# Linear attention and a tanh-shrink MLP on one core: batch 1 inside layer 2 of chunk 0 regrouped, kv on packed v, its last tokens in chunk 1

## The chip, the cores and the metric

The kernel runs on one core of one Trainium2 chip. The core has engines that run side by side, each with its own in-order queue: PE (matmuls; PEld is its weight load), DVE (vector), ACT (scalar and activation), POOL (GpSimd) and SP (which here only issues DMAs). POOL issues DMAs too. The metric is the device time of one execution in microseconds. The kernel before takes 285.66 us, the median of three runs (285.46 to 286.16).

## The reference

Inputs q, k and v have the shape (8 batches, 8 heads, 576 tokens, 64). Linear attention with phi(x) = elu(x) + 1 is followed by a two-layer MLP with g = h - tanh(h):

```python
q_p, k_p = (phi(q), phi(k))
kv  = einsum('bhsd,bhse->bhde', k_p, v)          # 64 x 64 for each head
z   = sum(k_p, axis=2)                           # 64 for each head
num = einsum('bhsd,bhde->bhse', q_p, kv)
den = einsum('bhsd,bhd->bhs', q_p, z)[..., None] + 1e-06
x   = (num / den) as (4608 tokens, 512)
h   = x @ w_in                                   # 512 x 2048
out = (h - tanh(h)) @ w_out                      # 2048 x 512
```

## The kernel before, in words

**Tiles.** The 4608 tokens are worked through in nine chunks `c` of 512. A chunk has layer 1 (16 tiles `fi` of 128 hidden features, four matmuls of 128x512 each, L425) and layer 2 (four blocks of 128 tokens, sixteen matmuls each, L446). After a pair of layer-1 tiles ACT takes the tanh (L431) and DVE subtracts (L432, into `gT`); in chunk 0 this is done for single tiles (L436, L437). ACT copies a finished layer-2 block out of PSUM (`evac`, L455) and SP stores it (L466). A batch has 576 tokens, so chunks and batches don't line up: chunk 1 holds tokens 512 to 1023, which are the last 64 tokens of batch 0 and the first 448 of batch 1; chunk 2 begins with the last 128 of batch 1.

**Attention.** For a batch, phi of q and k is an exponential on ACT (L131), a `max, add` on DVE (L132) and a minimum on DVE (L133), twice for each tensor (i = 0, 1, pairs of heads). q is then transposed, by PE through `ident` for batches 0 and 1 (L161, copied out by ACT L165 and DVE L167), by a DMA on SP for the later ones (L150). kv is 72 matmuls in 64x64 tiles (`kv_mm`, L179). z comes with it as further columns: for batch 1 (`a_kv`, L182) the moving operand is a 64-column piece of v and a 64-column piece of ones, which lie in a third slot of `v_b[1]` (128 columns, written by the POOL memset L484); for the batches from 2 on (`kv_cols_mm`, L194) it is a packed copy `vp` of v, 64 columns of v and two of ones (66 columns), made by DVE (`a_vp`, L192). `kz_copy` (or the end of `a_kv`) takes kv and the masked z to SBUF on DVE. `a_den` makes the denominators (16 matmuls L330, an add L335 and a reciprocal L339 on DVE). `num_mm` (L267) makes the numerators of the first 512 tokens of a batch, in 64x512, and `rest_mm` (L275) those of the last 64, in 64x64.

**Scaling by 1/den.** The reciprocals are spread over the partitions. Batch 0 does this with fp32 selection matmuls (L294) for the first 512 tokens and with a round trip through DRAM for its last 64 (`b0_rest`: four stores and two broadcast loads on SP, L307 and L310; `scale_rest`, L317). Batch 1 splits the reciprocals into bf16 parts on DVE (`a_split`, L349 to L352), spreads all 576 by bf16 selection matmuls (`a_spread_pe`, L413) in two halves, and multiplies (`a_scale`, L418) with the numerators, which ACT has copied to `ns` (L584 for the last 64 tokens, L588). Batch 2 goes through DRAM (`a_spread`, L359, L362), the later batches scale q itself.

**What sets the order.** The order of each engine's work is the order of the calls, written out by hand. `s1[fi]` and `s2[s]` are lists of things to do after layer-1 tile `fi` and after layer-2 step `s` of a chunk. In layer 2 of chunk 0 a step `s` is `(g, i) = divmod(s, 4)`: group g of four features, step i; a step has four matmuls. The loads of q, k and v are issued on POOL (L91), and since `kraw` and `qraw` have one buffer, the next batch's load waits until phi of the present one has read it. All eight PSUM banks are one tile, `ps_all`; layer 2 of chunk 0 accumulates in banks 0 to 3, so that batch 1 has banks 4 to 7; layer 1 of chunk 1 takes banks `fi % 6`. The steps that matter here, in chunk 0:

```python
s2[4]  a_qphi(1, 1), load_q(2), load_k(2), load_v(2)
s2[7]  a_qT_pe(1, 0, banks 4, 5), a_kv(1, 6), a_qT_pe(1, 1, banks 4, 5)
s2[8]  scale_rest(0, 6, ..), a_den(1, 4), num1(), a_split(1)
s2[10] spread1(0)
s2[11] exp2(q of batch 2, half 0)
s2[12] spread1(1), exp2(q, half 1), rest2(q, half 0)
s2[13] exp2(k, half 0), rest2(q, half 1), a_qT_dma(2)
s2[14] rest2(k, half 0)
```

`exp2` is the exponential on ACT and `rest2` the two DVE steps. After steps 12 to 15 comes the `evac` of a finished block, ahead of the things in the list. In layer 1 of chunk 1: `s1[0]` a gate on POOL (L442) that waits for the transposed q of batch 2, and the loads of batch 3; `s1[1]` phi of the second half of k; `s1[3]` `a_vp(2, ..)`; `s1[8]` `kv_cols_mm(2, 6, 0)` and `kz_copy(2, 6, 0)` (L202, L207); `s1[10]` `a_den(2, 6)` and `a_spread(2)`.

Of the kernel before, what the change touches and what calls it, by code (L numbers as in the profile page):

```python
# [12 lines left out]
BF16 = mybir.dt.bfloat16  # L13
# [5 lines left out]
def kernel(  # L19
# [9 lines left out]
    nc = tc.nc  # L29
    B, H, S, D = q.shape  # L30
# [43 lines left out]
    w_out_sb = const.tile([128, NF, DM], BF16, name="w_out_sb")  # L74
    kz_c = [const.tile([128, 2, 2, 96], BF16, name=f"kz{i}") for i in range(2)]

    v_b = [const.tile([128, 3, 2, J, D], BF16, name=f"v{i}") for i in range(2)]
    vp = const.tile([128, 2, J, 2, 66], BF16, name="vp")


# [2 lines left out]
    def load(b, t, src, halves):  # L83

        x = src[b].rearrange("h (p j) d -> (h p) (j d)", j=J)
        if halves:
            for i in range(2):
                nc.gpsimd.dma_start(out=t[:, :, i].rearrange("q h j d -> q h (j d)"),  # L88
                                    in_=x.rearrange("(h i q) x -> i q h x", h=2, i=2)[i])
        else:  # L90
            nc.gpsimd.dma_start(out=t.rearrange("q h i j d -> q (h i) (j d)"),  # L91
                                in_=x.rearrange("(n q) x -> q n x", n=4))
# [5 lines left out]
    def load_q(b):  # L98
        q_t[b] = kpool.tile([128, 2, 2, J, D], BF16, name="qraw")
        load(b, q_t[b], q, b == 0)  # L100

    def load_v(b):
        load(b, v_b[b % 2][:, 0:2], v, b == 0)

    def load_wi(f0, n):

# [35 lines left out]
    def a_qphi(b, i):  # L142
        phi(b, q_t, qp_t, "qp", i)
# [29 lines left out]
    def kv_mm(b, v_of, ps_of):  # L173

        kp = kp_t[b]
        for i in range(2):
            for j in range(J):
                for rs, cs, hg, h in quads():
                    nc.tensor.matmul(ps_of(cs, hg, i), kp[rs, i, j, h, :], v_of(rs, h, i, j),  # L179
                                     start=(j == 0), stop=(j == J - 1))  # L180

    def a_kv(b, b0):  # L182

        kz_t[b], vt = kz_c[b % 2], v_b[b % 2]
        kv_mm(b, lambda rs, h, i, j: vt[rs, h:3:2 - h, i, j, :],
              lambda cs, hg, i: ps_all[cs, b0 + hg, 128 * i:128 * i + 128].rearrange("p (a e) -> p a e", a=2))
        ps = ps_all[:, b0:b0 + 2, 0:256].rearrange("p g (i e) -> p g i e", i=2)
        nc.vector.tensor_mul(kz_t[b][:, :, :, 64:96], ps[:, :, :, 64:96], mask)
        nc.vector.tensor_copy(kz_t[b][:, :, :, 0:64], ps[:, :, :, 0:64])

    def a_vp(b, i):
        nc.vector.tensor_copy(vp[:, i, :, :, 0:64].rearrange("p j h d -> p h j d"), v_b[b % 2][:, 0:2, i])  # L192

    def kv_cols_mm(b, b0, o):  # L194
        kz_t[b] = kz_c[b % 2]
# [104 lines left out]
            ns[:, p, j0:j1].rearrange("p j (t c) -> p t j c", t=4),  # L300
            ps_all[:, 4:8, 128 * n + 16 * j0:128 * n + 16 * j1].rearrange("p t (j c) -> p t j c", c=16))

    def b0_rest():

        ds = dram.tile([H, 4, 16], F32, name="ds0")
        for t in range(4):
            nc.sync.dma_start(out=ds[:, t, :], in_=rden_t[0][32 * t:32 * t + H, 128:144])  # L307
        rdb = rpool.tile([128, NP, 4, 16], F32, name="rdb0")
        for hh in range(2):
            nc.sync.dma_start(  # L310
                out=rdb[64 * hh:64 * hh + 64].rearrange("p a t c -> p (a t c)"),
                in_=ds[4 * hh:4 * hh + 4].rearrange("h t c -> (h t c)").partition_broadcast(64))
        rdb_t[0] = rdb

    def scale_rest(b, b0, rdb):
        for h, ps in enumerate(rest_mm(b, b0, 0)):
            nc.vector.tensor_mul(  # L317
                xT[:, 2 * h:2 * h + 2, S * b + 512:S * b + 576].rearrange("p a (t c) -> p a t c", t=4),
                ps.rearrange("p a (t c) -> p a t c", t=4), rdb[:, 2 * h:2 * h + 2])
# [84 lines left out]

        return rpool.tile([128, NP, J, 64], F32, name="ns", tag="rdb")

    def a_spread_pe(b, bank0, pairs):

        bp = ps_all[:, bank0:bank0 + 4, :]
        for n, p in enumerate(pairs):  # L410
            for t in range(4):
                r = slice(32 * t, 32 * t + 32)
                nc.tensor.matmul(bp[:, t, 144 * n:144 * n + 144], sel3[r, p].rearrange("p h e -> p (h e)"),  # L413
                                 rden_t[b][r], start=True, stop=True)
        return bp

    def a_scale(b, p, ns, bp, o):
        nc.vector.tensor_mul(  # L418
            xT[:, p, S * b:S * b + S].rearrange("p (j t c) -> p t j c", j=J, t=4),
            ns[:, p].rearrange("p j (t c) -> p t j c", t=4),  # L420
            bp[:, :, o:o + 144].rearrange("p t (j c) -> p t j c", c=16))


    def l1mm(c, fi, h, p, n):
# [24 lines left out]
    def evac(c, i, o, f0=0, f1=None):  # L449
        f1 = DM if f1 is None else f1  # L450
        osb = opool.tile([128, DM], F32, name="osb")
        if f0:
            nc.vector.tensor_copy(osb[:, f0:f1], o[:, f0:f1])  # L453
        else:
            nc.scalar.copy(osb[:, f0:f1], o[:, f0:f1])  # L455

        if c == NC - 1 and i == 3:
            nc.sync.dma_start(
                out=out[(B - 1) * S:, f0:f1].rearrange("(p j) m -> p j m", j=J)[:, J - 2:J],
                in_=osb[:, f0:f1])  # L460
            return
        for half in range(2):
            b, j = divmod(2 * (4 * c + i) + half, J)
            cuts = [f0, 256, f1] if c == 3 and i < 3 else [f0, f1]
            for a0, a1 in zip(cuts, cuts[1:]):
                nc.sync.dma_start(  # L466
                    out=out[b * S:(b + 1) * S, a0:a1].rearrange("(p j) m -> p j m", j=J)[:, j, :],
                    in_=osb[64 * half:64 * half + 64, a0:a1])
# [12 lines left out]
    load_wo(0)  # L481
    load_wo(1)
    load_q(1)
    nc.gpsimd.memset(v_b[1][:, 2], 1.0)  # L484
    nc.gpsimd.memset(vp[:, :, :, :, 64:66], 1.0)
    load_v(1)
    for n in range(2):
# [51 lines left out]
    b0_kz(0)  # L539
    a_den(0, 4)  # L540
    ns0 = new_ns(0)
    b0_rest()
    b0_num(0)
    b0_kv(1)
    b0_kz(1)
# [22 lines left out]
    for c in range(NC):  # L568
# [4 lines left out]
        if c == 0:  # L573
            sub = {}

            def spread1(h):
                sub["bp"] = a_spread_pe(1, 4, (2 * h, 2 * h + 1))
                for p in (2 * h, 2 * h + 1):
                    a_scale(1, p, sub["ns"], sub["bp"], 144 * (p % 2))

            def num1():
                ns = sub["ns"] = new_ns(1)
                for h, ps in enumerate(rest_mm(1, 6, 128)):
                    nc.scalar.copy(ns[:, 2 * h:2 * h + 2, 8, :], ps)  # L584
                for i in range(2):
                    b0 = 4 + 2 * i
                    num_mm(1, i, lambda h: b0 + h)
                    nc.scalar.copy(ns[:, i::2, 0:8, :].rearrange("p a j t -> p a (j t)"), ps_all[:, b0:b0 + 2, :])  # L588

            s1[11].append(lambda: a_kphi(1, 0))  # L590
            s1[13].append(lambda: a_kphi(1, 1))
            s2[3].append(lambda: a_qphi(1, 0))
            s2[4].append(lambda: (a_qphi(1, 1), load_q(2), load_k(2), load_v(2)))
            s2[0].append(prepare)
            s2[7].append(lambda: (a_qT_pe(1, 0, Banks([4, 5])), a_kv(1, 6), a_qT_pe(1, 1, Banks([4, 5]))))
            s2[8].append(lambda: (scale_rest(0, 6, rdb_t[0]), a_den(1, 4), num1(), a_split(1)))
            s2[10].append(lambda: spread1(0))

            qs, ks = [], []

            def exp2(pieces, src, store, name, i):
                pieces.append(phi_pieces(2, src, store, name, i))
                pieces[i][0]()

            def rest2(f):
                f[1]()
                f[2]()

            s2[11].append(lambda: exp2(qs, q_t, qp_t, "qp", 0))
            s2[12].append(lambda: (spread1(1), exp2(qs, q_t, qp_t, "qp", 1), rest2(qs[0])))  # L610
            s2[13].append(lambda: (exp2(ks, k_t, kp_t, "kp", 0), rest2(qs[1]), a_qT_dma(2)))
            s2[14].append(lambda: rest2(ks[0]))
        elif n1 < B:
            if c == 1:
                s1[8].append(lambda: (kv_cols_mm(2, 6, 0), kz_copy(2, 6, 0)))
            if n1 < QS:
                s1[10].append(lambda: (a_den(n1, 6), a_spread(n1)))
            else:
                if c == 2:
                    s1[2].append(lambda: (q_den(n1, 0, 0), q_den(n1, 0, 1)))  # L620
                e = 2 * (c == 2)
                s1[3 + e].append(lambda: q_den(n1, 1, 0))
                s1[5 + e].append(lambda: q_den(n1, 1, 1))
                s1[7 + e].append(lambda: q_scale(n1))
            m = 12 if c == 1 else 9
            s2[m].append(lambda: a_num(n1, n2 if n2 < B else 0))
            if n2 < B:
                s2[m + 2].append(lambda: (q_zb(n2, 4 if c == 1 else 7), q_prod(n2)))
                if c > 1:
                    s2[15].append(lambda: (q_den(n2, 0, 0), q_den(n2, 0, 1)))  # L630
# [100 lines left out]
```

## Time and profile before

| what | value |
|---|---|
| median of three runs | 285.66 us |
| profiled execution, its own time | 285.88 us |
| span in its profile | 284.1 us |
| PE busy | 277.1 us, 98% |
| DVE busy | 175.8 us, 62% |
| ACT busy | 146.6 us, 52% |
| POOL busy | 74.1 us, 26% |
| granted PE clock | full speed in every slice |
| L446 and L425, layers 2 and 1 | 560 matmuls each, 124.6 and 122.7 us busy |
| L179, kv of batch 1 (128 columns) / of a later batch (66) | 72 matmuls: 1.13 us / 0.71 us in the chain |
| L484, memset of the ones beside v | 1.08 us on POOL |

The span is the profiled execution from its first to its last instruction; what lies around it, 1.8 us here, is the difference to its own time. A "busy" share is an average over the whole span. A chain of work that ended last is followed back from the end, so a stretch of it that names one engine without gaps says that this engine set the pace there. Lines such as `L446` are lines of the kernel before; in the tables of groups, the number behind "x" counts instructions.

### The profile page before, as it was taken

Reading aid. Unit: us, or ns where it says so; the run is one execution under the profiler, and the core shown is the slowest. Engines: PE = TensorE matmul, PEld = TensorE weight load, DVE = VectorE, ACT = ScalarE, POOL = GpSimd, SP = SyncE. Lnnn points to the kernel's source line nnn. Section 1 sums busy time; section 2 is a strip of 40 time slices with the busy share of each in tenths; the row PEclk is TensorE's granted clock in tenths of the full one; section 3 lists DMA queues with packets and bytes.
Section 4 is the critical chain, followed back from the end, with each engine's and each line's share of the span. In section 5 each row is a group of like instructions: output and inputs, shape, how many; then the busy total and the mean of one; then the engine's idle time right before and its main releaser. Section 6 shows DMA issues by size and latency. Waiting matters only on the chain.

```text
span 284.1 us, 5104 instructions
## 1 busy us (share of the span) xinstructions
PE 277.1 (98%) x2099; PEld 131.8 (46%) x2099; DVE 175.8 (62%) x279; ACT 146.6 (52%) x179; POOL 74.1 (26%) x66
## 2 busy tenths in 40 slices
PE   8879999999999999999999999999999999999995
PEld 3564464444444454445444444444444444444443
DVE  5748977997479773976397648764770267006600
ACT  3738658847445663667355736663551355126411
POOL 8652030020360536143605360505050000000000
PEclk9999999999999999999999999999999999999999
DMA  6999999997992299037913693141105210230032
GB/s 99 192 206 213 207 207 207 245 171 141 228 234 69 52 203 221 9 85 131 235 34 70 109 223 85 40 111 45 37 16 119 61 37 2 52 79 18 2 74 74
DMA packets 38343, 32.99 MB, mean 116 GB/s; under 512 B 16016, under 2 KB 34096, under 8 KB 38192
## 3 DMA queue, kind: packets, MB, share of 16 engines
q0 software_dynamic: 17488, 18.35, 39.9%
q1 hardware_dynamic: 20832, 14.31, 20.0%
q8 instruction: 16, 0.26, 0.4%
q14 instruction: 7, 0.06, 0.1%
HBM read 38.01 MB, written 9.46 MB: 167 GB/s over the span
## 4 chain that ended last, share of the span: by engine, by line
PE 90%; DMA 5%; POOL 1%; DVE 1%; ACT 1%; issue 1%; SPq 0%; DVEq 0%; POOLq 0%
PE ps_all L425 43%; PE ps_all L446 40%; DMA v<-in_v_dram 3%; DMA out_dram<-osb 2%; PE ps_all L179 2%; PE ps_all L267 2%; PE ps_all L653 1%; DVE xT L298 1%; ACT osb L455 1%; SPq L466 0%; POOL kraw L88 0%; POOL qraw L88 0%; PE ps_all L330 0%; PE ps_all L294 0%; PE ps_all L161 0%
## 5 line engine op out<-in xcount | busy, mean ns | idle before, releaser
L446 PE MATMUL ps_all<-w_out_sb,gT 128*128 128x512 bf16 x560 | 124.6, 379 | 0.0
L425 PE MATMUL ps_all<-xT,w_in_sb 128*128 128x512 bf16 x560 | 122.7, 379 | 0.0
L432 DVE TENSOR_TENSOR gT<-ps_all,th 128x1024 bf16<-128x1024 f32 x64 | 77.7, 1217 | 46.7 <-ACT th L431 46.7
L431 ACT ACTIVATE th<-ps_all 128x1024 f32<-128x1024 f32 x64 | 65.6, 1024 | 48.2 <-PE ps_all L425 47.5
L425 PEld LDWEIGHTS <-w_in_sb 128*128 128x128 bf16 x560 | 54.6, 98 | 65.6
L446 PEld LDWEIGHTS <-gT 128*128 128x128 bf16 x560 | 53.8, 98 | 63.3 <-issue 0.2
L455 ACT COPY osb<-ps_all 128x512 f32<-128x512 f32 (+1 forms) x36 | 20.9, 583 | 56.4 <-PE ps_all L446 42.2
L238 POOL TENSOR_TENSOR qp<-qp,rd 128x1152 bf16<-128x1152 bf16 x10 | 21.0, 2117 | 39.1 <-issue 23.7
L224 POOL TENSOR_TENSOR pr<-qp,zb 128x1152 f32<-128x1152 bf16 x10 | 23.4, 2359 | 23.9 <-ACT zb L217 23.9
L131 ACT ACTIVATE e<-qraw 128x1152 bf16<-128x1152 bf16 x16 | 18.5, 1160 | 7.0 <-DMA qraw<-in_q_dram 7.0
L229 DVE TENSOR_REDUCE dn<-pr 128x9 f32<-128x576 f32 x20 | 14.5, 745 | 12.2 <-POOL pr L224 12.2
L131 ACT ACTIVATE e<-kraw 128x1152 bf16<-128x1152 bf16 x15 | 17.4, 1162 | 0.4 <-DMA kraw<-in_k_dram 0.4
L133 DVE TENSOR_TENSOR qp<-e,r 128x1152 bf16<-128x1152 bf16 x16 | 12.1, 758 | 4.9 <-ACT e L131 4.1
L133 DVE TENSOR_TENSOR kp<-e,r 128x1152 bf16<-128x1152 bf16 x15 | 11.4, 758 | 6.1 <-ACT e L131 5.1
L91 POOL DMA_DIRECT2D kraw<-in_k_dram x7 | 5.4, 770 | 28.9 <-ACT e L131 26.2
L437 DVE TENSOR_TENSOR gT<-ps_all,th 128x512 bf16<-128x512 f32 x16 | 10.3, 685 | 3.1 <-ACT th L436 2.5
L436 ACT ACTIVATE th<-ps_all 128x512 f32<-128x512 f32 x16 | 9.2, 598 | 5.7 <-PE ps_all L653 4.5
L91 POOL DMA_DIRECT2D qraw<-in_q_dram x7 | 5.4, 768 | 23.8 <-DVE r L132 13.3
L517 PE MATMUL ps_all<-zero 128*128 128x512 bf16 x29 | 8.9, 466 | 1.2 <-DVE zero L471 1.2
L132 DVE TENSOR_SCALAR r<-qraw 128x1152 bf16<-128x1152 bf16 x16 | 7.4, 461 | 0.5 <-DMA qraw<-in_q_dram 0.5
L453 DVE COPY osb<-ps_all 128x128 f32<-128x128 f32 x1 | 0.3, 291 | 11.6 <-DMA out_dram<-osb 11.6
L132 DVE TENSOR_SCALAR r<-kraw 128x1152 bf16<-128x1152 bf16 x15 | 6.8, 451 | 0.0
(103 smaller groups left out, 137.7 us busy)
## 6 DMA issues: line engine op xcount, KB each, us to landing
out_dram<-osb SPq DMA_DIRECT2D x64, 128.0 KB, 2.4
kraw<-in_k_dram POOLq DMA_DIRECT2D x7, 576.0 KB, 6.5
qraw<-in_q_dram POOLq DMA_DIRECT2D x7, 576.0 KB, 8.4
v<-in_v_dram POOLq DMA_DIRECT2D x7, 576.0 KB, 11.3
w_in_sb<-in_moe_w_in_dram POOLq DMA_DIRECT2D x3, 512.0 KB, 13.7
w_out_sb<-in_moe_w_out_dram POOLq DMA_DIRECT2D x3, 512.0 KB, 18.7
rdb<-ds SPq DMA_DIRECT2D x2, 576.0 KB, 7.8
out_dram<-osb SPq DMA_DIRECT2D x13, 64.0 KB, 4.4
```

What stands on the lines that cost most here:

```text
L91: nc.gpsimd.dma_start(out=t.rearrange("q h i j d -> q (h i) (j d)"), in_=x.rearrange("(n q) x -> q n x", n=4))
L131: return (lambda: nc.scalar.activation(e, x, AF.Exp), lambda: nc.vector.tensor_scalar(r, x, 0.0, 1.0, ALU.max, ALU.add), lambda: nc.vector ...
L132: lambda: nc.vector.tensor_scalar(r, x, 0.0, 1.0, ALU.max, ALU.add),
L133: lambda: nc.vector.tensor_tensor(y, e, r, ALU.min))
L224: nc.gpsimd.tensor_mul(pr_t[b][:, i].rearrange("p j h d -> p j (h d)"), qp_t[b][:, i].rearrange("p j h d -> p j (h d)"), zb_t[b][:, i].uns ...
L229: nc.vector.tensor_reduce(dn_t[b][:, i, :, h], pr_t[b][:, i, :, h, :], mybir.AxisListType.X, ALU.add)
L238: nc.gpsimd.tensor_mul(x, x, rd[:, i].unsqueeze(2).to_broadcast([128, J * 2, D]))
L425: nc.tensor.matmul(h, w_in_sb[:, p, fi * 128:(fi + 1) * 128], xT[:, p, c * 512:(c + 1) * 512], start=(n == 0), stop=(n == NP - 1))
L431: nc.scalar.activation(th, h, AF.Tanh)
L432: nc.vector.tensor_sub(gT[:, fi:fi + 2, :], h, th)
L446: nc.tensor.matmul(o, gT[:, fi, i * 128:(i + 1) * 128], w_out_sb[:, fi, :], start=(fi == 0), stop=(fi == NF - 1))
L455: nc.scalar.copy(osb[:, f0:f1], o[:, f0:f1])
```

## The change

Batch 1's work inside layer 2 of chunk 0 is regrouped. Both halves of q are transposed in one go (into banks 4, 5 and 6, 7). kv then runs on packed v (`vp`, 66 columns) in banks 4 and 5, as it does for the later batches; the packing is done by two copies on POOL, in the step that holds the loads of batch 2 and ahead of them in POOL's queue. The third slot of `v_b` and its memset go. Batch 0's last 64 tokens are multiplied right behind this kv, in other columns of the same banks. den and num of batch 1 stand together in step 8, num with its second half first. Batch 1's last 64 tokens are no longer computed here: their reciprocals go through DRAM (`spread_rest(1)`, six DMAs on SP, as for batch 0), and their matmuls and scaling stand beside kv of batch 2 in chunk 1. The spread is one block of 16 matmuls of 128 columns after step 11, where there were two of 8 with 144 columns after steps 10 and 12. In chunk 3 the store of the last block is cut in two column halves as those of the other blocks are.

```diff
-    v_b = [const.tile([128, 3, 2, J, D], BF16, name=f"v{i}") for i in range(2)]
+    v_b = [const.tile([128, 2, 2, J, D], BF16, name=f"v{i}") for i in range(2)]
...
-    def a_kv(b, b0):
...
-    def a_vp(b, i):
-        nc.vector.tensor_copy(vp[:, i, :, :, 0:64].rearrange("p j h d -> p h j d"), v_b[b % 2][:, 0:2, i])
+    def a_vp(b, i, eng=nc.vector):
+        eng.tensor_copy(vp[:, i, :, :, 0:64].rearrange("p j h d -> p h j d"), v_b[b % 2][:, :, i])
...
-    def b0_rest():
+    def spread_rest(b):
...
-            nc.sync.dma_start(out=ds[:, t, :], in_=rden_t[0][32 * t:32 * t + H, 128:144])
+            nc.sync.dma_start(out=ds[:, t, :], in_=rden_t[b][32 * t:32 * t + H, 128:144])
...
-    def scale_rest(b, b0, rdb):
-        for h, ps in enumerate(rest_mm(b, b0, 0)):
+    def scale_rest(b, pss):
+        rdb = rdb_t[b]
+        for h, ps in enumerate(pss):
...
-    def a_spread_pe(b, bank0, pairs):
+    def a_spread_pe(b, pairs):
...
-                nc.tensor.matmul(bp[:, t, 144 * n:144 * n + 144], sel3[r, p].rearrange("p h e -> p (h e)"),
-                                 rden_t[b][r], start=True, stop=True)
+                nc.tensor.matmul(ps_all[:, 4 + t, 128 * n:128 * n + 128], sel3[r, p].rearrange("p h e -> p (h e)"),
+                                 rden_t[b][r, 0:128], start=True, stop=True)
...
-            cuts = [f0, 256, f1] if c == 3 and i < 3 else [f0, f1]
+            cuts = [f0, 256, f1] if c == 3 else [f0, f1]
...
-    nc.gpsimd.memset(v_b[1][:, 2], 1.0)
...
-            def spread1(h):
-                sub["bp"] = a_spread_pe(1, 4, (2 * h, 2 * h + 1))
-                for p in (2 * h, 2 * h + 1):
-                    a_scale(1, p, sub["ns"], sub["bp"], 144 * (p % 2))
+            def spread1():
+                a_spread_pe(1, range(NP))
+                for p in range(NP):
+                    a_scale(1, p, sub["ns"], p)
+
+            def kv1():
+                kv_cols_mm(1, 4, 0)
+                pss = rest_mm(0, 4, 256)
+                kz_copy(1, 4, 0)
+                scale_rest(0, pss)
...
-                for h, ps in enumerate(rest_mm(1, 6, 128)):
-                    nc.scalar.copy(ns[:, 2 * h:2 * h + 2, 8, :], ps)
-                for i in range(2):
+                for i in (1, 0):
...
-            s2[4].append(lambda: (a_qphi(1, 1), load_q(2), load_k(2), load_v(2)))
+            s2[4].append(lambda: (a_qphi(1, 1), a_vp(1, 0, nc.gpsimd), a_vp(1, 1, nc.gpsimd), load_q(2), load_k(2), load_v(2)))
...
-            s2[7].append(lambda: (a_qT_pe(1, 0, Banks([4, 5])), a_kv(1, 6), a_qT_pe(1, 1, Banks([4, 5]))))
-            s2[8].append(lambda: (scale_rest(0, 6, rdb_t[0]), a_den(1, 4), num1(), a_split(1)))
-            s2[10].append(lambda: spread1(0))
+            s2[7].append(lambda: (a_qT_pe(1, 0, Banks([4, 5])), a_qT_pe(1, 1, Banks([6, 7])), kv1()))
+            s2[8].append(lambda: (a_den(1, 4), num1(), spread_rest(1), a_split(1)))
+            s2[11].append(spread1)
...
-            s2[12].append(lambda: (spread1(1), exp2(qs, q_t, qp_t, "qp", 1), rest2(qs[0])))
+            s2[12].append(lambda: (exp2(qs, q_t, qp_t, "qp", 1), rest2(qs[0])))
...
-                s1[8].append(lambda: (kv_cols_mm(2, 6, 0), kz_copy(2, 6, 0)))
+                def kv2():
+                    kv_cols_mm(2, 6, 0)
+                    pss = rest_mm(1, 6, 256)
+                    kz_copy(2, 6, 0)
+                    scale_rest(1, pss)
+
+                s1[8].append(kv2)
```

More of the change, by code (lines that the diff above doesn't have):

```diff
@@ L102, in load_v @@
     def load_v(b):
-        load(b, v_b[b % 2][:, 0:2], v, b == 0)
+        load(b, v_b[b % 2], v, b == 0)
     def load_wi(f0, n):
@@ L180, in kv_mm @@
                                      start=(j == 0), stop=(j == J - 1))
-    def a_kv(b, b0):
[L184 to L189, printed above, removed]
-    def a_vp(b, i):
-        nc.vector.tensor_copy(vp[:, i, :, :, 0:64].rearrange("p j h d -> p h j d"), v_b[b % 2][:, 0:2, i])
+    def a_vp(b, i, eng=nc.vector):
+        eng.tensor_copy(vp[:, i, :, :, 0:64].rearrange("p j h d -> p h j d"), v_b[b % 2][:, :, i])
     def kv_cols_mm(b, b0, o):
@@ L312, in b0_rest @@
                 in_=ds[4 * hh:4 * hh + 4].rearrange("h t c -> (h t c)").partition_broadcast(64))
-        rdb_t[0] = rdb
-    def scale_rest(b, b0, rdb):
-        for h, ps in enumerate(rest_mm(b, b0, 0)):
+        rdb_t[b] = rdb
+    def scale_rest(b, pss):
+        rdb = rdb_t[b]
+        for h, ps in enumerate(pss):
             nc.vector.tensor_mul(
@@ L405, in new_ns @@
         return rpool.tile([128, NP, J, 64], F32, name="ns", tag="rdb")
-    def a_spread_pe(b, bank0, pairs):
-        bp = ps_all[:, bank0:bank0 + 4, :]
+    def a_spread_pe(b, pairs):
         for n, p in enumerate(pairs):
@@ L412, in a_spread_pe, with a_scale @@
                 r = slice(32 * t, 32 * t + 32)
-                nc.tensor.matmul(bp[:, t, 144 * n:144 * n + 144], sel3[r, p].rearrange("p h e -> p (h e)"),
-                                 rden_t[b][r], start=True, stop=True)
-        return bp
-    def a_scale(b, p, ns, bp, o):
+                nc.tensor.matmul(ps_all[:, 4 + t, 128 * n:128 * n + 128], sel3[r, p].rearrange("p h e -> p (h e)"),
+                                 rden_t[b][r, 0:128], start=True, stop=True)
+    def a_scale(b, p, ns, n):
         nc.vector.tensor_mul(
-            xT[:, p, S * b:S * b + S].rearrange("p (j t c) -> p t j c", j=J, t=4),
-            ns[:, p].rearrange("p j (t c) -> p t j c", t=4),
-            bp[:, :, o:o + 144].rearrange("p t (j c) -> p t j c", c=16))
+            xT[:, p, S * b:S * b + 512].rearrange("p (j t c) -> p t j c", j=8, t=4),
+            ns[:, p, 0:8].rearrange("p j (t c) -> p t j c", t=4),
+            ps_all[:, 4:8, 128 * n:128 * n + 128].rearrange("p t (j c) -> p t j c", c=16))
     def l1mm(c, fi, h, p, n):
@@ L541 @@
     ns0 = new_ns(0)
-    b0_rest()
+    spread_rest(0)
     b0_num(0)
```

## The prediction, made before the change was run

> **What bounds the kernel now.** I read the page's busy rows first, then the chain of work that ended last, in order of time, around the edited blocks, then the timeline of all engines there, and last the DMA issues with their landings.
>
> ```profile
> PE   8879999999999999999999999999999999999995
> ...
> PE 90%; DMA 5%; POOL 1%; DVE 1%; ACT 1%; issue 1%; SPq 0%; DVEq 0%; POOLq 0%
> ```
>
> PE is busy in every slice but the first few, and the chain is PE for 90% of the span: from 21 us on, PE work taken away shortens the kernel, unless a wait takes its place. The chain through the edited stretch (start, length, what):
>
> ```profile
> 38.55 0.50 PE ps_all L161 x9
> 39.05 1.13 PE ps_all L179 x72
> 40.18 0.61 PE ps_all L161 x9
> 40.79 0.86 PE ps_all L446 x4
> 41.66 0.19 PE ps_all L275 x8
> 41.84 0.36 PE ps_all L330 x16
> ...
> 42.43 0.25 PE ps_all L275 x7
> 42.69 0.92 PE ps_all L267 x8
> 43.61 1.83 PE ps_all L446 x8
> 45.44 0.24 PE ps_all L413 x8
> 45.67 1.83 PE ps_all L446 x8
> 47.51 0.24 PE ps_all L413 x8
> 47.74 2.70 PE ps_all L446 x12
> ```
>
> The reader is to see the seven interruptions of L446 (layer 2) and what each costs. But PE is not alone here. In the timeline (start, length, engine, and in brackets the idle time before and its releaser) the other engines stand close behind:
>
> ```profile
> 38.64 0.74 POOL L91 DMA_DIRECT2D qraw<-in_q_dram  x1 [13.29 <-DVE r L132]
> 46.34 1.16 ACT L131 ACTIVATE e<-qraw 128x1152 bf16<-128x1152 bf16 x1 [1.27 <-DMA qraw<-in_q_dram]
> 50.62 1.07 ACT L455 COPY osb<-ps_all 128x512 f32<-128x512 f32 x2
> 52.20 1.02 ACT L431 ACTIVATE th<-ps_all 128x1024 f32<-128x1024 f32 x1 [0.51 <-PE ps_all L425]
> 53.26 1.22 DVE L432 TENSOR_TENSOR gT<-ps_all,th 128x1024 bf16<-128x1024 f32 x1 [0.35 <-ACT th L431]
> 60.14 0.41 DVE L207 CAST kz<-ps_all 128x256 bf16<-128x256 f32 x1
> 60.68 0.43 PE L330 MATMUL ps_all<-qT,kz 128*32 128x144 bf16 x16
> ```
>
> ACT waits for q of batch 2, issued at 38.64 and landing at 46.24 (7.6 us). From 46.34 it works without a gap to 51.69 (5.35 us: three exponentials, four evacuations), then idles only 0.51 us before chunk 1's first tanh. That releases DVE at 53.26, which has no gap until kz of batch 2 is done at 60.55; PE's den of batch 2 starts 0.13 us later. So this second chain has 0.51 us of room at the tanh, and about 0.1 us at den.
>
> **PE's work.** A layer-2 matmul takes 6.91/32 = 0.216 us. From 38.55 to 50.44 stand 32 of them, 6.91 of 11.89 us; the blocks cost 4.98. After the change: 18 transposes in one run, 2 x 0.50 = 1.00 (the 0.61 held a switch); kv on packed v, 72 of 66 columns, 0.71 (the L179 block at 58.21 in chunk 1); eight rest matmuls beside it, 0.06 (between 77.15 and 77.21); den 0.36; num 0.56 (the eight at 76.76; here they now take 0.92, with waits); one spread. Eight of 144 columns take 0.24, of which 2 groups x 144 x 0.00042 = 0.12 is columns (0.216/512 each), so sixteen of 128 take 0.12 + 4 x 0.054 = 0.34. Three returns to layer 2 cost 1.83 - 8 x 0.216 = 0.10 each. Sum 1.00 + 0.77 + 0.92 + 0.34 + 0.30 = 3.33, a saving of 1.65; batch 1's rest in chunk 1 gives back 0.06. PE alone: **-1.59 us**.
>
> **What the packed v adds.** Two copies of 128x1152 on POOL now stand between v's landing and kv, and ahead of the issue of q, k and v of batch 2 in POOL's queue. v of batch 1, issued at 17.05, lands 21.2 us later, at 38.25. Dropping the memset (1.08 us at 15.96) moves its issue up by a microsecond but not its landing: transfers on this queue land in order, 576 KB every 2.84 us (q 35.43, v 38.25), at 207 GB/s in every slice here. So POOL cannot start before 38.3, and PE, which began kv at 39.05, is to read the copies.
>
> No POOL copy of this size is in the trace. Below stands the memset of the same size, 1.08 us, which writes and reads nothing; above the POOL product of the same size (L238), 2.12, which reads two inputs. I take 1.1, nearer the memset because a copy reads one stream, and keep both ends. The start: DVE's minimum (L133) runs 38.22 to 38.98 with both inputs in SBUF. The nearest row on sharing is DVE's copy of v (L192): median 0.454, but 0.58 at 71.38 and 0.65 at 100.47, each beside a POOL DMA issue. I take 0.2 us of delay (bounds 0 and 0.7): start 38.45, copies done 39.55 and 40.65.
>
> The Trainium skill (SBUF — State Buffer, "Who interferes with whom") says that a VectorE instruction with two SBUF inputs and a GpSimd one that reads SBUF exclude each other for the whole instruction; by it the copies would start at 38.98 and the end be 286.5. The Trainium skill (GPSIMD Engine Reference, 3.1) gives 1.8 cycles an element at 1.2 GHz for a tight loop, an estimate of 1.73 us a copy, and the end 287.2; its 4.1 calls one-input work roughly line-rate, as the memset row has it. No run here shows either yet.
>
> PE: transposes end at 39.55; first half of kv to 40.0; the second half waits for 40.7. That stall of 0.7 us, and 0.1 before num's last half (bank 4 is read by den's add, behind two scalings on DVE), leave 0.8 of the 1.59.
>
> **What follows from POOL.** q's issue starts at 40.65 plus 0.34, the gap after a POOL copy (55.87 + 0.18 to 56.39): 41.0, not 38.64. Behind it in the queue are k and v of batch 2. An issue that finds the queue empty lands 6.2 us later (k of batch 3, 56.39); q of batch 0 in halves, 4.6 + 1.4 for the second half's bytes, gives 6.0. With 6.1, q lands at 47.1; the queue's order would have allowed 46.24 (weights until 43.4, plus 2.84). So the delay is 0.9 us. ACT's 5.35 us then run 47.2 to 52.55, the tanh starts at 52.6 (0.4 late), DVE's chain ends 0.4 late, and den of batch 2, with its 0.1 of room, starts **0.3 us later** than now, whatever PE saved ahead of it. Nothing gives this back: after den PE runs without idle time to the end.
>
> With d for one copy, the end moves by 2d - 1.9 us, and by no less than -0.6: q cannot land before 46.24, which leaves 0.5 at the tanh and 0.1 at den.
>
> **The rest.** The two scalings moved to chunk 1 (2 x 0.285 on DVE, behind kz) meet 0.43 us of idle time before the next subtraction, so 0.14 us is late, and later idle times of 0.32 and 0.50 take it; without that cover 0.57. The six small DMAs of the rest go to SP near 43.8. Its pair of batch 0 waited 3.5 us between stores and loads, and took 6.4 in all, so SP is free at 50.2 rather than 48.2. Behind it queue four output stores and the transpose of q (51.76), perhaps 1 us late. That holds the gate on POOL (55.87) and the loads of batch 3; q transposed is read at 60.68 and would land at 56.7; v of batch 3 (68.84, read at 69.00) would hold DVE 0.9 us where it later idles 0.89. Nothing for PE. ACT's two small copies of rest (0.43) go from a stretch in which it then waits 1.27. Two more stores in chunk 3 meet an SP that mostly waits. The scaling, 4 x 0.68 after a spread at 45.8, ends by 48.8, before chunk 1's layer 1.
>
> **Sum.** The profiled execution took 285.88 us (span 284.1). Plus 0.3 is 286.18; it stands 0.22 above the median of 285.66, so the forecast is **286.0**. A measurement can tell about 0.3% (0.86 us) from no change.
>
> **Rivals.** (A) The forecast: PE's saving is eaten by the later q, through ACT and DVE. With d 1.1, its ends come from start 38.3 to 38.98, gap 0 to 0.34, landing 5.7 to 6.2: from the floor of -0.6 (285.1) to +0.9 (286.5). Chance 0.55, within. (B) Slower: POOL's copies are slow, like its products. It decides from d = 1.4, where 2d - 1.9 passes 0.86; at 1.7 it is +1.5 (287.2), at 2.12 +2.3 (288.0); 287.6 in the middle. For it: every POOL arithmetic row is near 2 us; against: the memset. Chance 0.33, slower. (C) Faster: DVE and ACT run ahead and PE's saving comes through, 285.66 - 1.59 = 284.1. It needs q no later than now and 1 us that DVE's gapless stretch doesn't show. Chance 0.08. (D) The copies' reads hold DVE's minimum and the work behind it for a whole copy, 1.1 us on the path to transposes and so to kv, and the scalings in chunk 1 lose their cover, 0.14: 286.9. Chance 0.04, slower.
>
> The range leaves out C and the upper edge of B, and takes in the floor of A: 285.0 to 287.9. A alone: 285.1 to 286.5. Faster 0.08, same 0.55, slower 0.37.
>
> **What will show it.** In the changed profile: two POOL copies near 38.4, with their length; kv's second half held by them; the issue of q near 41.0 and its landing near 47.1; no idle time of ACT before the first tanh, at 52.6; den of batch 2 held by DVE's kz. Layer 2 of chunk 0 is to end near 49.7, 0.8 sooner than now, and this gain is to be gone at den. Wrong would be copies of another length, a q that lands as before, or PE keeping its gain past 61 us.

## The result and the profile after

The changed kernel takes **287.1 us** (median of 22 runs, 285.5 to 288.6), the kernel before, run beside it, 285.81 (22 runs). The ratio is 1.0044, with a 95% interval of 1.0033 to 1.0056: 1.3 us slower. The profiled execution has a span of 285.4 us, 284.1 before. The measured time lies in the stated range of 285.0 to 287.9, but above the 286.5 at which the forecast's own rival (A) ended, and it is slower by more than 0.3%, where "within 0.3%" was held likeliest.

Line numbers of the kernel after differ: layer 1 is L415 (before L425), layer 2 L436 (L446), the evacuation L445 (L455), the tanh L421 (L431), the subtraction L422 (L432), the copy of v L183 (L192), kz L193 and L198 (L202, L207), the scaling of a batch's last 64 tokens L309 (L317), den L322 (L330), num L258 (L267), the spread L404 (L413).

The page of the changed kernel, first PE's busy tenths in 40 slices, then the chain that ended last:

```profile
PE   8879989899999999999999999999999999999995
...
PE 77%; DMA 10%; issue 6%; POOL 3%; ACT 2%; SPq 0%; DVE 0%; POOLq 0%; ACTq 0%
```

A digit is PE's busy share of one slice in tenths. Two slices (36 to 43 us and 50 to 57 us) fell from 9 to 8, and the chain has gone over to DMA and POOL for part of the way. The chain between 38 and 62 us says where (start, length, what):

```profile
38.39 0.08 POOL vp L183
...
39.96 1.09 POOL vp L183
41.05 7.26 DMA qraw<-in_q_dram
...
48.40 1.16 ACT e L131
49.56 0.47 ACT osb L445
50.03 1.06 ACT e L131
...
51.46 1.17 ACT e L131
52.64 0.48 ACT osb L445
...
53.16 6.20 PE ps_all L415 x28
```

It is to be read from the top: copies of v on POOL, the load of q issued behind them, ACT's exponentials and evacuations, and only then layer 1 on PE. The same stretch in the timeline (in brackets the idle time before, and its releaser):

```profile
38.39 2.71 POOL L183 COPY vp<-v 128x1152 bf16<-128x1152 bf16 x2 [12.93 <-DMA v<-in_v_dram]
41.05 0.74 POOL L91 DMA_DIRECT2D qraw<-in_q_dram  x1
48.40 1.16 ACT L131 ACTIVATE e<-qraw 128x1152 bf16<-128x1152 bf16 x1 [2.94 <-DMA qraw<-in_q_dram]
53.47 1.05 ACT L421 ACTIVATE th<-ps_all 128x1024 f32<-128x1024 f32 x1
40.07 0.48 PE L179 MATMUL ps_all<-vp,kp 64*64 64x66 bf16 x36 [0.32 <-POOL vp L183]
41.16 0.48 PE L179 MATMUL ps_all<-vp,kp 64*64 64x66 bf16 x36 [0.61 <-POOL vp L183]
50.38 1.03 PE L415 MATMUL ps_all<-xT,w_in_sb 128*128 128x512 bf16 x4
51.62 1.02 PE L415 MATMUL ps_all<-xT,w_in_sb 128*128 128x512 bf16 x4 [0.22 <-ACT osb L445]
53.16 6.20 PE L415 MATMUL ps_all<-xT,w_in_sb 128*128 128x512 bf16 x28 [0.52 <-ACT osb L445]
61.26 0.41 DVE L198 CAST kz<-ps_all 128x256 bf16<-128x256 f32 x1
61.59 0.48 DVE L309 TENSOR_TENSOR xT<-ps_all,rdb 128x128 bf16<-128x128 f32 x2
61.93 0.43 PE L322 MATMUL ps_all<-qT,kz 128*32 128x144 bf16 x16
```

q was issued at 41.05 (38.64 before) and landed at 48.31 (46.24). ACT's first tanh of chunk 1 starts at 53.47 (52.20), without idle time ahead of it. On PE the account is short. Transposes start at 38.41 (38.39 before), layer 1 at 50.38 (50.28): up to here the regrouping has won nothing. From layer 1 to den of batch 2 it is 11.55 us against 10.40. The eight matmuls from 50.38 to 53.16 take 2.78 us where 8 x 0.216 = 1.73 is their work, so **1.05 us** is waiting for ACT to empty banks 1 and 2; the rest of batch 1 is some 0.06. Together with the later start of layer 1 (0.10) that is 1.2; den is 1.25 us late, the span 1.3. From den to the end the two kernels take the same (223.5 us after, 223.4 before), so nothing behind it, the stores of chunk 3 included, has a share.

DVE arrives at den in the same moment. From its first subtraction in chunk 1 (54.56, behind the late tanh) it has no gap; kz is done at 61.67, and the first of the two scalings of batch 1's rest, which the change put behind kz, at 61.87, 0.06 us ahead of den. This scaling reads bank 6, into which den is to write, so den follows it.

### The profile page after: what moved, and what is told of

It reads as the page before. It is cut to its first block, busy times and chain, and to the rows that moved or that the text cites. A ratio compares the mean times of both kernels' runs of the same rounds, so it can differ in the third digit from the quotient of the medians.

```text
span 285.4 us, 5117 instructions
## 1 busy us (share of the span) xinstructions
PE 276.6 (97%) x2099; PEld 131.4 (46%) x2099; DVE 175.8 (62%) x281; ACT 145.9 (51%) x177; POOL 76.0 (27%) x67
## 4 chain that ended last, share of the span: by engine, by line
PE 77%; DMA 10%; issue 6%; POOL 3%; ACT 2%; SPq 0%; DVE 0%; POOLq 0%; ACTq 0%
PE ps_all L415 38%; PE ps_all L436 35%; DMA w_in_sb<-in_moe_w_in_dram 5%; DMA qraw<-in_q_dram 3%; DMA out_dram<-osb 2%; PE ps_all L179 1%; ACT e L131 1%; PE ps_all L258 1%; POOL w_in_sb L107 1%; ACT osb L445 1%; POOL v L88 1%; SPq L456 0%; POOL kraw L88 0%; POOL qraw L88 0%; POOL vp L183 0%
## 5 line engine op out<-in xcount | busy, mean ns | idle before, releaser
L436 PE MATMUL ps_all<-w_out_sb,gT 128*128 128x512 bf16 x560 | 124.5, 379 | 0.0
L415 PE MATMUL ps_all<-xT,w_in_sb 128*128 128x512 bf16 x560 | 123.0, 379 | 0.7 <-ACT osb L445 0.7
L422 DVE TENSOR_TENSOR gT<-ps_all,th 128x1024 bf16<-128x1024 f32 x64 | 77.8, 1218 | 47.2 <-ACT th L421 47.0
L421 ACT ACTIVATE th<-ps_all 128x1024 f32<-128x1024 f32 x64 | 65.6, 1025 | 47.6 <-PE ps_all L415 45.3
L415 PEld LDWEIGHTS <-w_in_sb 128*128 128x128 bf16 x560 | 54.6, 98 | 66.6 <-issue 1.3
L436 PEld LDWEIGHTS <-gT 128*128 128x128 bf16 x560 | 53.8, 98 | 63.4 <-issue 0.2
L445 ACT COPY osb<-ps_all 128x512 f32<-128x512 f32 (+1 forms) x36 | 20.9, 583 | 56.3 <-PE ps_all L436 40.0
L427 DVE TENSOR_TENSOR gT<-ps_all,th 128x512 bf16<-128x512 f32 x16 | 10.3, 686 | 3.8 <-ACT th L426 3.1
```

What stands on the lines that cost most here:

```text
L415: nc.tensor.matmul(h, w_in_sb[:, p, fi * 128:(fi + 1) * 128], xT[:, p, c * 512:(c + 1) * 512], start=(n == 0), stop=(n == NP - 1))
L421: nc.scalar.activation(th, h, AF.Tanh)
L422: nc.vector.tensor_sub(gT[:, fi:fi + 2, :], h, th)
L436: nc.tensor.matmul(o, gT[:, fi, i * 128:(i + 1) * 128], w_out_sb[:, fi, :], start=(fi == 0), stop=(fi == NF - 1))
```

## Experiments

Each was timed in five rounds beside the kernel before. Theory 1, the late q, says that the loss is the load of q behind two POOL copies. The first rival says that it is PE's wait for these copies ahead of kv, the second that it is batch 1's rest, through SP and DVE.

**The late q alone, on the kernel before.** The copies are made and nobody reads them.

```diff
-            s2[4].append(lambda: (a_qphi(1, 1), load_q(2), load_k(2), load_v(2)))
+            s2[4].append(lambda: (a_qphi(1, 1), a_vp(1, 0, nc.gpsimd), a_vp(1, 1, nc.gpsimd), load_q(2), load_k(2), load_v(2)))
```

> The kernel before, with the two POOL copies of v put ahead of the loads of batch 2 and read by nobody: kv stays on unpacked v, so PE waits for no copy. Theory 1 (the late q): q is issued near 41.05 instead of 38.64 and lands near 48.3, ACT's gapless run ends 2 us later, the first tanh of chunk 1 starts near 53.5 and den of batch 2 some 1.2 us later than before: 1.2 us slower than before (ratio 1.004). Rival (PE's wait for the copies ahead of kv is the loss): no difference to before (1.000).

Measured: 1.0037 (1.0024 to 1.0051), 286.91 us beside 285.67. Its timeline, with the line numbers of the kernel before and the old kv of 128 columns that waits for no copy:

```profile
38.52 1.20 PE L179 MATMUL ps_all<-v,kp 64*64 64x128 bf16 x72
40.88 0.74 POOL L91 DMA_DIRECT2D qraw<-in_q_dram  x1
48.29 1.16 ACT L131 ACTIVATE e<-qraw 128x1152 bf16<-128x1152 bf16 x1 [3.69 <-DMA qraw<-in_q_dram]
49.98 1.02 PE L425 MATMUL ps_all<-xT,w_in_sb 128*128 128x512 bf16 x4
51.52 1.02 PE L425 MATMUL ps_all<-xT,w_in_sb 128*128 128x512 bf16 x4 [0.52 <-ACT osb L455]
53.06 6.20 PE L425 MATMUL ps_all<-xT,w_in_sb 128*128 128x512 bf16 x27 [0.52 <-ACT osb L455]
```

The same two waits for the evacuations stand in a kernel whose blocks are the old ones. The late q costs about 1.1 us by itself, and PE's wait ahead of kv has no part in it.

**The wait ahead of kv without the late q.** Raw q gets a second buffer, and the loads stand ahead of the copies.

```diff
-        q_t[b] = kpool.tile([128, 2, 2, J, D], BF16, name="qraw")
+        q_t[b] = kpool.tile([128, 2, 2, J, D], BF16, name="qraw", bufs=2)
...
-            s2[4].append(lambda: (a_qphi(1, 1), a_vp(1, 0, nc.gpsimd), a_vp(1, 1, nc.gpsimd), load_q(2), load_k(2), load_v(2)))
+            s2[4].append(lambda: (a_qphi(1, 1), load_q(2), load_k(2), load_v(2), a_vp(1, 0, nc.gpsimd), a_vp(1, 1, nc.gpsimd)))
```

> The changed kernel with a second buffer for raw q and the three loads of batch 2 ahead of the two POOL copies: PE still waits for the copies ahead of kv, q is not late. Theory 1 (the late q): q lands near 46.2, the loss goes; what is left is PE, whose layer 1 of chunk 1 starts near 50.4 as in both kernels, so 0 to 0.2 us faster than before (ratio 0.999 to 1.000). Rival (PE's wait ahead of kv): slower than before by as much as the change, 1.004.

Measured: 1.0012 (0.9993 to 1.0031), 285.83 beside 285.67. q is there in time, and no loss shows, though PE waits as long ahead of kv (0.94 us; 0.32 and 0.61 in the changed kernel), for a reason that the timeline shows:

```profile
38.19 2.76 POOL L183 COPY vp<-v 128x1152 bf16<-128x1152 bf16 x2 [3.38 <-DMA v<-in_v_dram]
38.23 1.72 DVE L133 TENSOR_TENSOR qp<-e,r 128x1152 bf16<-128x1152 bf16 x1
40.00 0.68 PE L161 MATMUL ps_all<-ident,qp 128*128 128x128 bf16 x9 [0.94 <-DVE qp L133]
46.31 1.16 ACT L131 ACTIVATE e<-qraw 128x1152 bf16<-128x1152 bf16 x1 [1.00 <-DMA qraw<-in_q_dram]
```

The POOL copy began 0.04 us ahead of DVE's minimum, which took 1.72 us for 0.76. These two experiments part theory 1 from the first rival.

**Batch 1's rest without its DMAs.**

```diff
-            s2[8].append(lambda: (a_den(1, 4), num1(), spread_rest(1), a_split(1)))
+            s2[8].append(lambda: (a_den(1, 4), num1(), rdb_t.update({1: rdb_t[0]}), a_split(1)))
```

> The changed kernel without the six small DMAs of batch 1's rest on SP: the last 64 tokens of batch 1 are scaled with batch 0's reciprocals, so these 64 rows of the output are not the reference's; all other work is the same. Theory 1 (the late q): SP's output stores and the transpose of q go out about 2 us sooner, which nobody on PE's path waits for: 1.0044 as the changed kernel, within 0.1%. Rival (the rest through SP holds the transpose, the gate and the loads of batch 3): most of the 1.3 us goes, 1.000.

Measured: 1.0053 (1.0034 to 1.0072). The loss stays; the six DMAs on SP have no share that shows. The scaling in chunk 1 was still done here, so it alone was not taken away. But the kernel with the loads ahead and the next one hold the scaling and the six DMAs too, and neither shows the loss.

**The copies on DVE.**

```diff
-            s2[4].append(lambda: (a_qphi(1, 1), a_vp(1, 0, nc.gpsimd), a_vp(1, 1, nc.gpsimd), load_q(2), load_k(2), load_v(2)))
+            s2[4].append(lambda: (a_qphi(1, 1), load_q(2), load_k(2), load_v(2)))
...
-            s2[7].append(lambda: (a_qT_pe(1, 0, Banks([4, 5])), a_qT_pe(1, 1, Banks([6, 7])), kv1()))
+            s2[7].append(lambda: (a_vp(1, 0), a_qT_pe(1, 0, Banks([4, 5])), a_vp(1, 1), a_qT_pe(1, 1, Banks([6, 7])), kv1()))
```

> The changed kernel with its two copies of v on DVE, one ahead of each half of q's transposes' evacuation, so that POOL issues q as before. Theory 1 (the late q): q lands at 46.24 again, the first tanh starts near 51.7, den of batch 2 some 0.6 us earlier than in the kernel before: ratio 0.998 to before, 1.9 us faster than the changed kernel. Rival (PE's wait ahead of kv): the wait shrinks from 0.93 us to about 0.6, so only 0.3 us faster than the changed kernel, ratio 1.003. Rival (rest through SP and its scaling in chunk 1): no difference to the changed kernel, 1.0044.

Measured: 0.9996 (0.9986 to 1.0005), 285.69 beside 285.67. The loss goes, the gain of 0.6 us does not come. In the profiled execution q was issued at 38.93 and landed 8.4 us later, at 47.30, not 46.24; ACT's run was late by as much, and PE again stood before bank 2.

**Can PE's saving be collected?** Two edits to the changed kernel move what stands between q and PE. One puts the packing of batch 2's v on POOL, out of DVE's gapless stretch:

```diff
-            s2[14].append(lambda: rest2(ks[0]))
+            s2[14].append(lambda: (rest2(ks[0]), a_vp(2, 0, nc.gpsimd), a_vp(2, 1, nc.gpsimd)))
...
-            s1[3].append(lambda: (a_vp(2, 0), a_vp(2, 1)))
```

> The changed kernel with the packing of batch 2's v on POOL (behind phi of k) instead of DVE in chunk 1, which takes 0.82 us out of DVE's gapless stretch ahead of kz of batch 2. Theory 1a (the late q reaches PE through the late evacuations of banks 1 and 2, for which PE stands still 1.05 us in layer 1 of chunk 1; DVE's kz is done 0.26 us before den asks): no difference to the changed kernel, ratio to before 1.0044. Theory 1b (the prediction's road: it reaches PE through DVE and kz at den): 0.3 to 0.8 us faster than the changed kernel, 1.002 to 1.003.

The other puts two evacuations ahead of an exponential:

```diff
-            s2[13].append(lambda: (exp2(ks, k_t, kp_t, "kp", 0), rest2(qs[1]), a_qT_dma(2)))
-            s2[14].append(lambda: rest2(ks[0]))
+            s2[13].append(lambda: (rest2(qs[1]), a_qT_dma(2)))
+            s2[15].append(lambda: (exp2(ks, k_t, kp_t, "kp", 0), rest2(ks[0])))
```

> The changed kernel with the exponential of k's first half and its DVE steps behind the last two evacuations of chunk 0 instead of ahead of them, so that banks 2 and 3 come free 1.06 us sooner; q is as late as in the changed kernel and the first tanh starts as late. Theory 1a (banks): PE's stand before the third tile goes, but DVE's kz, done at 61.7, lies only 0.2 us behind that bank wait, so den is reached at about 61.8: 0.1 to 0.3 us faster than the changed kernel, 1.0035 to 1.004. Theory 1b (DVE alone): no difference, 1.0044.

Then both together, with the POOL packing also in `s2[15]`, and both with batch 1's copies on DVE as above:

> The changed kernel with both: evacuations first, and batch 2's packing on POOL. Theory 1a with DVE close behind it: only both together free PE, which reaches den of batch 2 near 61.0 instead of 61.97: about 1 us faster than the changed kernel, 1.001 to before. If one wait alone were the road, this would be no better than the better of the two single edits.

> The changed kernel with batch 1's copies on DVE, so that q is issued as before, and both reliefs of the preceding kernel. The PE stand of 0.74 us that is left with the copies on DVE alone goes: den of batch 2 some 0.5 us earlier than in the kernel before, ratio 0.998 to before. If PE's saving of 1.59 us were not real, no better than 1.000.

Measured: packing on POOL 1.0062 (1.0039 to 1.0085); evacuations first 1.0045 (1.0028 to 1.0063); both 1.0070 (1.0049 to 1.0092); both with the copies on DVE 1.0015 (0.9998 to 1.0033). The pair was to give back 1 us and gave nothing; the last was to come to 0.998 and missed as well. The packing on POOL turned out to be no relief. From the kernel with both edits and late q (an execution of 286.67 us, where the median of its six is 287.55):

```profile
53.27 2.24 POOL L183 COPY vp<-v 128x1152 bf16<-128x1152 bf16 x2 [10.26 <-DMA v<-in_v_dram]
54.67 1.15 DVE L132 TENSOR_SCALAR r<-kraw 128x1152 bf16<-128x1152 bf16 x1
57.88 0.81 PE L415 MATMUL ps_all<-xT,w_in_sb 128*128 128x512 bf16 x3 [0.66 <-DVE gT L422]
```

DVE's tensor_scalar beside the POOL copies takes 1.15 us for 0.45, the subtraction behind it is late, and PE waits 0.66 us for that. So the times of these four do not part the two roads from q to PE (evacuated banks, or DVE's chain at den): the first edit put back on DVE what it took off. In the last of the four the same happened (1.28 for 0.45, and a wait of 0.39 us on PE), so it doesn't decide either whether PE's saving is real.

The profile of the kernel with the evacuations first says more. q landed later still (48.69 us); PE waited 0.52 us for bank 1, no longer for bank 2, and 0.37 for a subtraction. Den comes right behind the first scaling (61.96 to 62.24) all the same:

```profile
61.96 0.48 DVE L309 TENSOR_TENSOR xT<-ps_all,rdb 128x128 bf16<-128x128 f32 x2
62.29 0.43 PE L322 MATMUL ps_all<-qT,kz 128*32 128x144 bf16 x16
```

From the landing of q to den it is 13.60 us here and 13.62 in the changed kernel, 13.61 without the rest's DMAs and 13.60 with the copies on DVE, whether PE waited for one bank or for two. In all four DVE works without a gap from the first subtraction of chunk 1 to the scaling, which ends 0.05 to 0.06 us ahead of den. So the road through DVE would have held den by itself; the waits for banks run beside it.

**The four blocks one step apart**, with copies on DVE and the second buffer of q:

```diff
-            s2[7].append(lambda: (a_qT_pe(1, 0, Banks([4, 5])), a_qT_pe(1, 1, Banks([6, 7])), kv1()))
-            s2[8].append(lambda: (a_den(1, 4), num1(), spread_rest(1), a_split(1)))
-            s2[11].append(spread1)
+            s2[7].append(lambda: (a_vp(1, 0), a_qT_pe(1, 0, Banks([4, 5])), a_vp(1, 1), a_qT_pe(1, 1, Banks([6, 7]))))
+            s2[8].append(kv1)
+            s2[9].append(lambda: (a_den(1, 4), num1(), spread_rest(1), a_split(1)))
...
-            s2[12].append(lambda: (exp2(qs, q_t, qp_t, "qp", 1), rest2(qs[0])))
+            s2[12].append(lambda: (spread1(), exp2(qs, q_t, qp_t, "qp", 1), rest2(qs[0])))
```

> The changed kernel with batch 1's copies on DVE, a second buffer for raw q (q of batch 2 is issued ahead of time), and the four blocks set one layer-2 step apart: transposes after step 7, kv after step 8, den and num after step 9, spread after step 12. This is to show whether PE's saving of 1.59 us exists once no copy and no DVE step is waited for. If so, layer 1 of chunk 1 starts 1.3 to 1.6 us sooner than in the kernel before, counted from the start of the transposes (11.89 us there, 10.3 to 10.6 here); the total then goes by the walls behind it (evacuations on ACT, DVE's gapless stretch): 0 to 0.5 us faster than before, 0.998 to 1.000. If the saving isn't real, the stretch stays near 11.3.

Measured: 0.9997 (0.9988 to 1.0007), 285.56 beside 285.84: the same time. The stretch from the transposes to layer 1 takes 11.65 us (38.13 to 49.78), not 10.3 to 10.6. Kv waits for no copy now, but two other things are late (the second row is layer 2 waiting for its own weights):

```profile
39.20 0.68 PE L161 MATMUL ps_all<-ident,qp 128*128 128x128 bf16 x9 [0.41 <-DVE qp L133]
40.15 1.02 PE L436 MATMUL ps_all<-w_out_sb,gT 128*128 128x512 bf16 x4 [0.28 <-DMA w_out_sb<-in_moe_w_out_dram]
```

Of the 1.41 us above the sum of 10.24, 1.02 lie up to this layer-2 step and 0.39 ahead of den and in num, as in the changed kernel. v, q and these weights come over one queue, which moves some 207 GB/s without a hole through this stretch in the kernel before; that this queue keeps PE from running ahead is argued from these two waits, not shown by a run.

Layer 1 does start 0.50 us sooner than in the kernel before (49.78 for 50.28), 0.26 of them because the transposes did. At den it is gone: DVE's kz is done at 60.57 (60.55 before), the first scaling at 60.77, and den starts at 60.83 (60.68). The second chain of the prediction holds it.

**The walls moved.** On top of this kernel both halves of phi of batch 2's k go to `s1[1]` and `s1[3]` of chunk 1, its kv to `s1[9]`, its den to `s1[11]`; the packing of v is once on POOL, once on DVE (this one is shown):

```diff
-            s2[13].append(lambda: (exp2(ks, k_t, kp_t, "kp", 0), rest2(qs[1]), a_qT_dma(2)))
-            s2[14].append(lambda: rest2(ks[0]))
+            s2[13].append(lambda: (rest2(qs[1]), a_qT_dma(2)))
...
-            s1[1].append(lambda: a_kphi(2, 1))
-            s1[3].append(lambda: (a_vp(2, 0), a_vp(2, 1)))
+            s1[1].append(lambda: a_kphi(2, 0))
+            s1[3].append(lambda: (a_kphi(2, 1), a_vp(2, 0), a_vp(2, 1)))
...
-                s1[8].append(kv2)
+                s1[9].append(kv2)
...
-                s1[10].append(lambda: (a_den(n1, 6), a_spread(n1)))
+                s1[11].append(lambda: (a_den(n1, 6), a_spread(n1)))
```

> The preceding kernel with the walls moved as well: both exponentials of batch 2's k in layer 1 of chunk 1 (after the tiles 1 and 3), its packing on POOL behind chunk 0, kv of batch 2 after tile 9 and its den after tile 11. If PE's saving is eaten by evacuations behind ACT's exponentials and by DVE ahead of kv of batch 2, it now comes through: 1.0 to 1.5 us faster than before, 0.995 to 0.9965. If POOL's copies hold DVE again, as with the packing on POOL before (DVE's tensor_scalar 1.1 us and more for 0.45), about 0.998.

> The preceding kernel with batch 2's packing on DVE behind phi of k instead of on POOL. DVE has 0.9 us more to do ahead of kv of batch 2, but nothing on POOL can hold it. If the shared port is what cost the kernels with the packing on POOL, this is as fast as or faster than its sister: 0.995 to 0.998.

Measured: 1.0051 (1.0034 to 1.0067) on POOL, 1.0025 (1.0014 to 1.0036) on DVE. Both expectations missed. On DVE (an execution of 287.19 us, its median is 286.38), kz of batch 2 is done at 62.53, the scaling behind it at 62.73, and PE waits 1.21 us for DVE ahead of den:

```profile
62.12 0.41 DVE L198 CAST kz<-ps_all 128x256 bf16<-128x256 f32 x1
62.79 0.43 PE L322 MATMUL ps_all<-qT,kz 128*32 128x144 bf16 x16 [1.21 <-DVE xT L309]
```

With phi of k later, DVE idles 0.45 us and then has the same work to do, so the second chain of the prediction is a wall of its own. The sister with the packing on POOL is slower by 0.7 us in the medians, as that expectation had it; DVE's tensor_scalar took 1.40 us for 0.45 there.

## Why the prediction was right, and where it failed

The mechanism of rival A, the forecast, is what happened: the load of q goes out behind two copies, lands late, and through ACT and DVE eats PE's saving. Its size was wrong: +0.3 us was added up, 1.3 measured, outside A's own range. That the stated range still holds the time is luck, since the upper part was taken in for copies that are slow by themselves (B), and they were not.

- **PE's work: the prices held, the waits didn't.** The spread took 0.34 (forecast 0.34) and the twelve matmuls ahead of it 2.69 (2.69). But from the transposes to layer 1 it is 11.97 us against a sum of 3.33 + 6.91 = 10.24. The 1.73 between: 0.66 until kv starts, 0.67 in kv, 0.23 ahead of den and 0.27 in den and num, less 0.10 for a return to layer 2 that cost nothing. Of this the prediction had a stall of 0.7 and 0.1 in num. "Leave 0.8 of the 1.59" failed; nothing was left. (The chain that the prediction shows has four interruptions of layer 2, with nine blocks in them, not seven; their sum of 4.98 is right.)
- **The copies.** 1.1 us was taken; undisturbed they take 1.14. The start was forecast 0.2 us late through sharing; the first copy took 1.63, 0.48 more, while DVE's minimum ran until 39.01 (least, median and most ns of the two copies in the first row):

```profile
L183 POOL COPY vp<-v x2: 1142/1384/1627, 38.4 to 40.0; 128x1152 bf16<-128x1152 bf16 x2
38.25 0.76 DVE L133 TENSOR_TENSOR qp<-e,r 128x1152 bf16<-128x1152 bf16 x1
```

  In the six profiles in which the minimum came first, the copy's excess is what was left of the minimum, less 0.13 to 0.14 each time: 0.62 left and 0.48 more here, 0.49 and 0.35 without the rest's DMAs, 0.31 to 0.33 and 0.17 to 0.19 in the other four. The Trainium skill (SBUF — State Buffer, "Who interferes with whom"), weighed against the row of DVE's copy, was the better guide: with the minimum first it was the copy that took longer, with the copy first the minimum (1.72). The 1.8 cycles an element of the Trainium skill (GPSIMD Engine Reference, 3.1), an estimate of 1.73 us a copy, did not hold here.
- **The issue of q** was forecast at 41.0 and came at 41.05: the copies were 0.45 later than thought, and the gap of 0.34 was not there.
- **The landing is the term that was mis-sized.** 6.1 us was taken, 7.26 came. One number stood for a spread: in the kernel before, the loads of k that find POOL's queue idle (batches 3, 5, 6, 7) land 6.2, 6.3, 6.5 and 6.1 us after their issue, in the changed one 7.4, 6.2, 6.4 and 6.4. The windows of one microsecond (the last two columns are the DMA engines' busy share and GB/s) show the hole, first after, then before:

```profile
42.00:43.00 1.00, 0.96 (x20) 0.43 (x17) 0.85 (x4) 0.00 (x0) 1.00 (x2) 1.00 0.90 73
43.00:44.00 1.00, 0.93 (x20) 0.36 (x10) 0.78 (x2) 0.47 (x1) 0.27 (x1) 1.00 0.67 90
```

```profile
42.00:43.00 1.00, 0.95 (x28) 0.47 (x17) 0.96 (x4) 0.28 (x2) 0.00 (x0) 1.00 1.16 195
43.00:44.00 1.00, 1.00 (x11) 0.44 (x7) 0.96 (x2) 1.00 (x2) 0.00 (x0) 1.00 1.23 208
```

  The DMA engines move less than half as much for two microseconds, although q was issued at 41.05. q therefore lands 2.07 us late, not 0.9, and the tanh starts 1.27 late, not 0.4. Put into the prediction's own sum (landing of q plus 5.5, less 52.20, less 0.1 of room), 48.31 gives +1.5; measured were 1.3.
- **The road.** That a late q eats PE's saving was right, and the two experiments on q bear it out. That it would do so through DVE at den holds too, with one step more than the prediction had: not kz (done at 61.67, 0.26 us before den) but the scaling behind it, done at 61.87, is what den follows. Beside this PE waited for evacuated banks, which the prediction did not have: I had read ACT's gapless run but not asked which banks its evacuations hold. In the changed kernel both come to the same moment; in the kernel with the evacuations first it is DVE.
- **The rest.** SP's DMAs cost nothing that shows, as forecast. The scaling was forecast to matter only for the next subtraction, but den waits for it: about 0.1 us where PE is there in time (0.26 from kz to den in the kernels one step apart and with the walls moved on DVE, 0.13 before). Rival B was wrong in its cause (the copies were not slow), though the time lies where it would have put copies of 1.6 us; D's mechanism, the copy holding DVE's minimum, came up in the kernel with the loads ahead.

What stays open: why the load took 7.3 us after its issue. No version that was run beats the kernel before; the best (0.9997 and 0.9996) equal it.

## What to carry to other kernels

An instruction set ahead of a load in an issuing engine's queue holds that load until it is done, its own waits included: the two copies, which waited for v, ran from 38.39 to 41.05, so a load that used to go out at 38.64 went out at 41.05. Where a busy queue is about to run dry, look at the landing, not at the issue: 2.4 us at the issue were 2.1 at the landing, and 1.1 to 1.3 of them arrived at PE. And work saved on the engine that sets the pace is only worth what the other engines' gapless stretches next to it allow; here 1.59 us of PE work stood behind a transfer, ACT, DVE and a queue of weights, and in no version that was run did any of it reach the end.

## What the runs showed of the hardware

A POOL copy of 128x1152 bf16 takes 1.14 us (the shorter copy of batch 1's two in seven profiles: 1.137 to 1.145). POOL and DVE hold each other up: the POOL copy takes up to 1.68 us behind DVE's minimum (longer by what is left of it, less 0.13 to 0.14), the minimum 1.72 for 0.76 behind the copy, a tensor_scalar 1.05 to 1.40 for 0.45 beside two copies. A load of 576 KB that POOL issues near 41 us, with the queue running dry, landed 6.5 to 7.8 us later in the six profiles in which the copies stand ahead of it. Four of these kernels are the same up to this point and show 6.5, 7.3, 7.7 and 7.7, so the moment varies by more than a microsecond from one execution to the next.
